# Linear attention and two feed-forward layers: the attention's two products in column halves

## The chip, the cores and the metric

The kernel runs on one core of a Trainium2 chip. The metric is the time of one execution on the device, in microseconds (us). The engines are named as the profile names them: PE is TensorE's matmuls and PEld its weight loads, DVE is VectorE, ACT is ScalarE, POOL is GpSimd, and SP is SyncE, which here only issues DMAs.

## What is computed

Attention with random features, with 4 sequences of 576 tokens, 8 heads of 64 and 128 features, then two feed-forward layers over the 2304 tokens, all of it in 32-bit floats:

```python
def phi(x):
    proj = np.einsum('bhsd,md->bhsm', x, omega)
    sq = np.sum(x * x, axis=-1, keepdims=True) / 2.0
    h = proj - sq
    h = h - np.max(h, axis=-1, keepdims=True)
    return np.exp(h) / np.sqrt(m)
q_p, k_p = (phi(q_s), phi(k_s))
kv = np.einsum('bhsm,bhsd->bhmd', k_p, v)
z = np.sum(k_p, axis=2)
num = np.einsum('bhsm,bhmd->bhsd', q_p, kv)
den = np.einsum('bhsm,bhm->bhs', q_p, z)[..., None] + 1e-06
return (num / den).astype(np.float32)
```

Then x is normed, goes through a gated layer (512 to 1536 to 512) and through a layer with h * cos(h) (512 to 2048 to 512). The two products that this case is about are kv with its sum z (from the keys' features and the values) and num with den (from the queries' features and kv).

## The kernel before

The 2304 tokens are 18 tiles of 128. A sequence has four and a half tiles, so tiles 4 and 13 each lie across two sequences; `parts(t)` gives the one or two pieces of a tile with their sequence, first partition and length.

A key tile goes this way. SyncE loads the transposed keys (`kraw`) and the values (`v`, one of three tiles, each 8 heads of 64 columns and one more column block that holds ones). `project` multiplies the keys by omega with two heads beside each other, in the upper and the lower 64 rows of the array (8 pairs of matmuls). `features` takes the maxima (DVE) and the exponentials (ACT, eight of them). `kv_product` then multiplies each head's features (stationary, 128 columns) by that head's values and the ones (moving, 64 + 64 columns), summed over a sequence in two banks of PSUM; `keep_kv` copies 65 of the 128 columns of each head to `kv`.

A query tile goes through eight steps, which `query_step` numbers: the projection and features, 1 the transposition of the features (`transposed`), 2 the products with kv (`sums`) and the division (`quotients`), 3 and 4 the mean square, 5 the norm, 6 and 7 the transposition into the layout of the first layer. In `sums` the transposed features of a head are stationary, and 128 columns of `kv` are moving, of which 65 are used later; a tile across two sequences does it in two halves of 64 tokens, each with its own `kv`.

The order on every engine is written out by hand: the program is a list of slots, and each engine does its instructions in the order in which the program issues them. In the key stage a slot s begins one tile (`begin(s)`) and does what older tiles are due for (`older(s, ...)`, whose arguments are the steps in their order; a key product has the number 1). There are 24 slots, with 18 key tiles and six query tiles. In the query stage the slots are the half steps of the first group of the first layer (`product`, `silu`, `gated`, `out1`), between which the remaining twelve query tiles are done.

Beside this the weights are prepared. They come as 64-bit floats and are turned into two parts of 32-bit words each: `front` makes a 32-bit value (its last step is an addition on POOL, L209), `high` casts its upper part (ACT, L214) and `low` subtracts it from the value (POOL, L217). The 12 pieces of the first group are made by `run` and `early_back`, while `self.early` is true; that ends with the key stage, and what is left of the twelve by then goes on with `self.early` false. `early_back` also asks for the piece after next but one, by a DMA from ACT's queue, right behind `high`.

Of the kernel before, what the change touches and what calls it, by code (L numbers as in the profile page):

```python
# [56 lines left out]
def attention_then_ffn(ctx: ExitStack, tc: tile.TileContext, qT, kT, v, omT, wc1, rms_g, wc2, out, B, H, S, D):  # L57
# [16 lines left out]
    IDLE = 9  # L74
    KVW = H * (D + 1) + D
    G = 4
# [50 lines left out]
    class Weights:  # L127
# [85 lines left out]
        def high(self, src, t, to):  # L213
            nc.scalar.copy(t[:, 0, to], src)  # L214

# [189 lines left out]
    class Attention:  # L405
# [51 lines left out]
        def sums(self, t, r):  # L457

            eT = self.eT.pop((t, r))
            ps = bank(self.tag, f"num_ps{t}_{r}")  # L460
            for h in range(HP):
                for b, p0, n in parts(t):
                    at = (2 * h + r) * (D + 1)
                    nc.tensor.matmul(
                        ps[p0:p0 + n, h * P:(h + 1) * P], eT[:, h, p0:p0 + n], self.kv[b][:, at:at + P],
                        start=True, stop=True, skip_group_check=True)
            self.ps["num", t, r] = ps
# [77 lines left out]
    with tc.manual_schedule():  # L545
# [20 lines left out]
        vp = values.enter_context(tc.tile_pool(name="values", bufs=1, side="right", reuse_waits="tile"))  # L566
        vt = [vp.tile([P, H + 1, D], F32, name=f"v{i}", bufs=1) for i in range(NV)]
        att = Attention(att_tile, "q", kv)
# [4 lines left out]
        def load_v(t):  # L573
            if t < NTILE:
                nc.sync.dma_start(vt[t % NV][:, 0:H], v[t])

        def kv_product(t, i):
# [3 lines left out]
            for r in range(2):  # L581
# [3 lines left out]
                for h in range(HP):  # L585
                    hh = 2 * h + r
                    nc.tensor.matmul(
                        acc[b, r][:, h * P:(h + 1) * P], att.e["k", t, r][p0:p0 + n, h, :],
                        vt[t % NV][p0:p0 + n, hh::H - hh, :],
                        start=begin and h == 0, stop=end, skip_group_check=True)  # L590
                if end:
# [199 lines left out]
        for a in vt:  # L791
            nc.vector.memset(a[:, H], 1.0)
        for a in kv:
            nc.vector.memset(a[:, H * (D + 1):], 0.0)
        make_identity(nc, ident)
# [4 lines left out]
        for s in range(SLOTS):  # L800
# [7 lines left out]
            begin(s)  # L808
            older(s, -7, -6, -4, -3, -2, -1, 1)
            if s:  # L810
# [138 lines left out]
        for n, (g, blk, f, first, last) in enumerate(steps):  # L949
# [13 lines left out]
            a = silu(blk, f, ps)  # L963
            older(s, -6, -4, -3, -2, -1)
            begin(s)
# [14 lines left out]
            hid[n] = gated(blk, f, a, ps)  # L980
            older(s + 1, -6, -4, -3, -2, -1)
            begin(s + 1)
# [447 lines left out]
```

## Time and profile before

| | |
|---|---|
| median of 3 runs | 964.47 us (964.46 to 966.03) |
| the profiled execution | 963.77 us |
| its span, from the first to the last instruction | 961.9 us |
| PE busy | 949.2 us, 99% of the span |
| DVE, ACT, POOL busy | 712.3, 536.9, 416.4 us |
| granted clock of TensorE | 0.999 of full speed over the span |

The time of an execution has 1.9 us around the span. A busy PE is not PE at its peak: matmuls are pipelined and overlap, so that the busy time of a group has the end of its last matmul in it, and the distance from one start to the next tells what one costs. A 32-bit matmul stands in the trace as two passes, each with a weight load of its own, so 8 matmuls are a row of 16.

### The profile page before, as it was taken

The numbers are of one execution on the slowest core, as the hardware profiler recorded it, in microseconds if no ns is written. First come the engines' busy times: TensorE is split into PE (matmuls) and PEld (weight loads), VectorE is DVE, ScalarE is ACT, GpSimd is POOL, SyncE is SP. The second block draws the span as 40 slices with busy tenths as digits, with TensorE's granted clock in tenths as the row PEclk, the third lists the DMA queues.
The fourth block names the chain that finished last, engine by engine and source line by source line (L and its number), as shares of the span: only waits on it lengthen the run. The fifth ranks groups of instructions, "written<-read, shape, count | busy, mean of one in ns | idle before, by whom it ended". The sixth has DMA issues, their size and how long they took to land. (4 is left out here: it accounts for less than half of the span.)

```text
span 961.9 us, 16225 instructions
## 1 busy us (share of the span) xinstructions
PE 949.2 (99%) x5761; PEld 892.0 (93%) x5761; DVE 712.3 (74%) x1163; ACT 536.9 (56%) x1155; POOL 416.4 (43%) x377
## 2 busy tenths in 40 slices
PE   9999999999999999999999999999999999999998
PEld 8998999989999999999999998888888889899897
DVE  5786677778863686577686648997799777786766
ACT  7787776775543524354453545575656565464443
POOL 2133367657944867275764673320244221230000
PEclk9999999999999999999999999999999999999999
DMA  8555178778697898846989794967622758307554
GB/s 313 157 181 187 57 265 293 256 265 263 219 328 291 328 330 295 302 152 197 376 303 377 249 348 152 345 231 271 208 88 79 272 186 303 125 23 269 197 226 162
DMA packets 96082, 227.65 MB, mean 237 GB/s; under 512 B 9728, under 2 KB 45184, under 8 KB 96000
## 3 DMA queue, kind: packets, MB, share of 16 engines
q1 hardware_dynamic: 94704, 222.34, 66.1%
q10 hardware_dynamic: 1296, 4.26, 1.2%
q8 instruction: 46, 0.75, 0.3%
q14 instruction: 36, 0.29, 0.1%
HBM read 156.04 MB, written 70.52 MB: 236 GB/s over the span
## 5 line engine op out<-in xcount | busy, mean ns | idle before, releaser
L1251 PE MATMUL o_ps<-w,o 128*128 128x512 f32 x864 | 226.0, 393 | 0.6 <-DVE o L1054 0.6
L209 POOL TENSOR_TENSOR f<-f,raw 128x512 f32<-128x512 f32 x68 | 94.7, 1393 | 230.3 <-DVE raw L204 184.6
L1251 PEld LDWEIGHTS o_ps<-w,o 128*128 128x128 f32 x864 | 159.7, 188 | 24.5 <-DVE o L1054 1.1
L217 POOL TENSOR_TENSOR w<-b,w 128x512 fp32r<-128x512 f32 x88 | 115.5, 1318 | 135.4 <-ACT w L214 125.6
L831 PE MATMUL gv_ps<-xhl,w 128*128 128x384 f32 x576 | 107.9, 335 | 1.6 <-DVE gv L870 1.1
L831 PEld LDWEIGHTS gv_ps<-xhl,w 128*128 128x128 f32 x576 | 100.5, 188 | 2.1 <-DVE gv L870 1.4
L1150 PE MATMUL y<-t,w 128*128 128x384 f32 x576 | 102.1, 334 | 0.3 <-POOL w L217 0.3
L1150 PEld LDWEIGHTS y<-t,w 128*128 128x128 f32 x576 | 100.0, 188 | 0.6 <-POOL w L217 0.6
L1051 ACT CAST o<-turns 128x384 fp32r<-128x384 f32 x96 | 47.5, 513 | 93.3 <-DVE turns L1232 93.3
L1043 PE MATMUL Xh<-T,w 128*128 128x384 f32 x432 | 87.4, 337 | 1.5 <-ACT h L1196 1.5
L1043 PEld LDWEIGHTS Xh<-T,w 128*128 128x128 f32 x432 | 76.8, 188 | 9.7 <-ACT h L1196 4.0
L1043 PE MATMUL X<-T,w 128*128 128x384 f32 x432 | 80.9, 335 | 0.0
L1043 PEld LDWEIGHTS X<-T,w 128*128 128x128 f32 x432 | 75.3, 188 | 0.5 <-DVE r L1078 0.3
L214 ACT CAST w<-b 128x512 fp32r<-128x512 f32 x88 | 50.5, 580 | 31.2 <-DVE b L274 23.9
L1054 DVE TENSOR_TENSOR o<-turns,o 128x384 fp32r<-128x384 f32 x96 | 59.9, 638 | 8.5 <-ACT o L1051 8.1
L884 PE MATMUL y_ps<-t,w 128*128 128x384 f32 x288 | 60.8, 346 | 0.0
L1017 ACT ACTIVATE turns<-turns,half_pi 128x768 f32<-128x768 f32 (+1 forms) x50 | 45.7, 914 | 22.4 <-DVE turns L1221 22.3
L1043 PE MATMUL Yh<-B,w 128*128 128x384 f32 x288 | 58.0, 336 | 0.0
L1221 DVE SCALAR_TENSOR_TENSOR turns<-turns,r 128x768 f32<-128x768 int32 (+1 forms) x50 | 56.4, 1128 | 1.7
L1232 DVE TENSOR_TENSOR turns<-h,turns 128x768 f32<-128x768 f32 (+1 forms) x50 | 54.8, 1096 | 2.4 <-ACT turns L1017 2.4
L1043 PEld LDWEIGHTS Yh<-B,w 128*128 128x128 f32 x288 | 51.4, 188 | 4.2 <-ACT h L1196 0.4
L190 DVE TENSOR_SCALAR f<-W 128x512 int32<-128x512 int32 x68 | 45.1, 663 | 13.6 <-ACT W L182 6.5
(117 smaller groups left out, 1853.6 us busy)
## 6 DMA issues: line engine op xcount, KB each, us to landing
T<-T_dram SPq DMA_DIRECT2D x48, 768.0 KB, 6.9
raw<-wc SPq DMA_DIRECT2D x60, 512.0 KB, 4.9
B<-yh_dram SPq DMA_DIRECT2D x21, 768.0 KB, 5.7
kept<-f SPq DMA_DIRECT2D x56, 256.0 KB, 5.0
b<-kept SPq DMA_DIRECT2D x56, 256.0 KB, 5.1
B<-x_dram SPq DMA_DIRECT2D x15, 768.0 KB, 6.6
x_dram<-xhl SPq DMA_DIRECT2D x12, 768.0 KB, 5.8
s<-x_dram SPq DMA_DIRECT2D x24, 384.0 KB, 6.3
```

The source lines that it names most:

```text
L209: nc.gpsimd.tensor_tensor(f32(f), f32(f), rest, op=ALU.add)
L214: nc.scalar.copy(t[:, 0, to], src)
L217: nc.gpsimd.tensor_tensor(t[:, 1, to], src, f32(t[:, 0, to]), op=ALU.subtract)
L831: nc.tensor.matmul(o, w[i], x[j], start=n == 0, stop=n == len(terms) - 1)
L884: nc.tensor.matmul(yacc[blk][e], w[:, i, e * P:(e + 1) * P], t[:, j], start=first and i + j == 0, stop=last and j == 1)
L1043: nc.tensor.matmul(o, w[:, i, c + kk * P:c + (kk + 1) * P], x[:, j, kk], start=begin and n == 0, stop=n == 5, skip_group_check=True)
L1051: nc.scalar.copy(t[:, 0], a)
L1054: engine.tensor_tensor(t[:, 1], a, f32(t[:, 0]), op=ALU.subtract)
L1150: nc.tensor.matmul(acc[e], w[:, i, e * P:(e + 1) * P], t[:, j], start=f == fs[0] and i + j == 0, stop=f == fs[-1] and j == 1)
L1221: nc.vector.scalar_tensor_tensor(r, a, -TWO_PI_LO, b, op0=ALU.mult, op1=ALU.add)
L1232: at(mu, lambda: nc.vector.tensor_tensor(r, h, r, op=ALU.mult))
L1251: nc.tensor.matmul(oacc[blk][j], o[:, x, js], w[:, y], start=first and n == 0, stop=last and n == 2)
```

## The change

Four things are edited.

- Both products go in two column halves. In `sums` the stationary features of a head are cut into tokens 0 to 63 and 64 to 127, in every tile; in `kv_product` the 128 features are cut likewise. Each half writes its own 64 partitions of PSUM. The moving operand has 65 columns, the head's 64 and the one of the sum.
- For that the tile of values has 65 columns a head, the last of them ones: the load writes 64 of 65 columns of each head. The memsets of the columns behind `kv`, which are no longer read, fall away.
- `high` casts on POOL and no longer on ACT, as long as `self.early` is true.
- In `older(...)` the steps -2 and -1 change places, at three calls.

```diff
-    KVW = H * (D + 1) + D
+    KVW = H * (D + 1)
...
         def high(self, src, t, to):
-            nc.scalar.copy(t[:, 0, to], src)
+            if self.early:
+                nc.gpsimd.tensor_copy(t[:, 0, to], src)
+            else:
+                nc.scalar.copy(t[:, 0, to], src)
...
             for h in range(HP):
-                for b, p0, n in parts(t):
-                    at = (2 * h + r) * (D + 1)
+                at = (2 * h + r) * (D + 1)
+                for c in range(2):
+                    half_c = slice(c * P // 2, (c + 1) * P // 2)
+                    b = parts(t)[min(c, len(parts(t)) - 1)][0]
                     nc.tensor.matmul(
-                        ps[p0:p0 + n, h * P:(h + 1) * P], eT[:, h, p0:p0 + n], self.kv[b][:, at:at + P],
+                        ps[half_c, h * P:h * P + D + 1], eT[:, h, half_c], self.kv[b][:, at:at + D + 1],
                         start=True, stop=True, skip_group_check=True)
...
-        vt = [vp.tile([P, H + 1, D], F32, name=f"v{i}", bufs=1) for i in range(NV)]
+        vt = [vp.tile([P, H, D + 1], F32, name=f"v{i}", bufs=1) for i in range(NV)]
...
-                nc.sync.dma_start(vt[t % NV][:, 0:H], v[t])
+                nc.sync.dma_start(vt[t % NV][:, :, 0:D], v[t])
...
-                    nc.tensor.matmul(
-                        acc[b, r][:, h * P:(h + 1) * P], att.e["k", t, r][p0:p0 + n, h, :],
-                        vt[t % NV][p0:p0 + n, hh::H - hh, :],
-                        start=begin and h == 0, stop=end, skip_group_check=True)
+                    for c in range(2):
+                        half_c = slice(c * M // 2, (c + 1) * M // 2)
+                        nc.tensor.matmul(
+                            acc[b, r][half_c, h * P:h * P + D + 1], att.e["k", t, r][p0:p0 + n, h, half_c],
+                            vt[t % NV][p0:p0 + n, hh, :],
+                            start=begin and h == 0, stop=end, skip_group_check=True)
...
         for a in vt:
-            nc.vector.memset(a[:, H], 1.0)
-        for a in kv:
-            nc.vector.memset(a[:, H * (D + 1):], 0.0)
+            nc.vector.memset(a[:, :, D:], 1.0)
...
-            older(s, -7, -6, -4, -3, -2, -1, 1)
+            older(s, -7, -6, -4, -3, -1, -2, 1)
```

The first place is on PE in the key stage, where the sums of the first query tile (`num_ps`) stand between a projection (`qp_ps`) and a key product (`kv_ps`), before:

```order
L426 MATMUL qp_ps_1_547<-om,qraw_421 128x128
L464 MATMUL num_ps_0_570<-kv_97,eT_0_498 128x128 x4
L464 MATMUL num_ps_1_580<-kv_97,eT_1_505 128x128 x4
L587 MATMUL kv_ps_0_447<-v_105,ke_0_520 128x128 x4
L587 MATMUL kv_ps_1_452<-v_105,ke_1_527 128x128 x4
L426 MATMUL kp_ps_0_602<-om,kraw_465 128x128
```

and after, where the shapes behind the names are those of one matmul's output:

```order
L429 MATMUL qp_ps_1_607<-om,qraw_457 128x128
L469 MATMUL num_ps_0_630<-kv_97,eT_0_550 64x65 x8
L469 MATMUL num_ps_1_644<-kv_97,eT_1_557 64x65 x8
L594 MATMUL kv_ps_0_483<-v_105,ke_0_572 64x65 x8
L594 MATMUL kv_ps_1_492<-v_105,ke_1_579 64x65 x8
L429 MATMUL kp_ps_0_678<-om,kraw_517 128x128
```

Nothing has changed its place, and each row of four matmuls became one of eight, all in halves, from the first of `num_ps` to the last of `kv_ps`.

The second place is on PE in the query stage, where a query tile's sums stand between two whole matmuls of the first layer (`gv_ps` and `y_ps`), before:

```order
L831 MATMUL gv_ps_1_0_1431<-xhl_0_774,w_795 128x384 x2
L831 MATMUL gv_ps_1_0_1431<-xhl_1_775,w_795 128x384 x2
L464 MATMUL num_ps_0_1446<-kv_98,eT_0_1393 128x128 x4
L464 MATMUL num_ps_1_1456<-kv_98,eT_1_1400 128x128 x4
L884 MATMUL y_ps_0_0_0_1465<-t_0_1382,w_417 128x384
L884 MATMUL y_ps_0_0_1_1466<-t_0_1382,w_417 128x384
```

and after:

```order
L836 MATMUL gv_ps_1_0_1619<-xhl_0_874,w_895 128x384 x2
L836 MATMUL gv_ps_1_0_1619<-xhl_1_875,w_895 128x384 x2
L469 MATMUL num_ps_0_1634<-kv_98,eT_0_1581 64x65 x8
L469 MATMUL num_ps_1_1648<-kv_98,eT_1_1588 64x65 x8
L889 MATMUL y_ps_0_0_0_1661<-t_0_1570,w_453 128x384
L889 MATMUL y_ps_0_0_1_1662<-t_0_1570,w_453 128x384
```

Here too the order is the same, but the halves now stand with 128-column matmuls on both sides. Seven of the twelve whole tiles of this stage are followed by a projection in place of `y_ps`.

The third place is POOL's first work on weights, where `f` is the 32-bit value and `w` the tile of its two parts, before:

```order
L209 TENSOR_TENSOR f_239<-f_239,raw_139 128x512
L217 TENSOR_TENSOR w_283<-f_239,w_283 128x512
L209 TENSOR_TENSOR f_281<-f_281,raw_172 128x512
L217 TENSOR_TENSOR w_367<-f_281,w_367 128x512
L209 TENSOR_TENSOR f_365<-f_365,raw_201 128x512
```

and after:

```order
L209 TENSOR_TENSOR f_243<-f_243,raw_139 128x512
L215 CAST w_295<-f_243 128x512
L220 TENSOR_TENSOR w_295<-f_243,w_295 128x512
L209 TENSOR_TENSOR f_293<-f_293,raw_168 128x512
L215 CAST w_395<-f_293 128x512
L220 TENSOR_TENSOR w_395<-f_293,w_395 128x512
L209 TENSOR_TENSOR f_393<-f_393,raw_197 128x512
```

A cast has come between the addition and the subtraction of a piece; there are eight such casts, and as many are gone from ACT. On ACT the DMA for a later piece stays where the cast stood before it.

## Rows read from the trace of the kernel before

**Rows 1.** First part of the page: busy us (share of the span) xinstructions.
```profile
PE 949.2 (99%) x5761; PEld 892.0 (93%) x5761; DVE 712.3 (74%) x1163; ACT 536.9 (56%) x1155; POOL 416.4 (43%) x377
```

**Rows 2.** Busy time by stretch: length; PE, PEld, DVE, ACT, POOL; clock, DMA, GB/s.
```profile
0.00:4.00 4.00, 2.90 (x9) 1.20 (x9) 0.84 (x9) 1.49 (x2) 0.84 (x9) 1.00 0.55 165
4.00:21.00 17.00, 16.70 (x173) 15.50 (x173) 11.16 (x21) 13.07 (x45) 4.16 (x3) 1.00 0.96 347
21.00:64.00 43.00, 42.85 (x438) 39.39 (x438) 33.42 (x70) 35.36 (x120) 11.75 (x13) 1.00 0.57 180
64.00:89.00 25.00, 24.33 (x255) 22.31 (x252) 19.37 (x44) 20.95 (x70) 8.96 (x8) 1.00 0.67 212
89.00:256.00 167.00, 164.06 (x1185) 158.77 (x1184) 126.48 (x255) 114.59 (x254) 108.50 (x114) 1.00 0.66 225
```

**Rows 3.** Timeline of a cycle in the key stage: start, length, what.
```profile
32.45 2.05 PE L464 MATMUL num_ps<-kv,eT 128*128 128x128 f32 x16
...
34.34 1.95 PE L587 MATMUL kv_ps<-v,ke 128*128 128x128 f32 x16
...
36.22 1.16 PE L426 MATMUL kp_ps<-om,kraw 64*128 64x128 f32 x16
...
37.31 1.09 PE L444 MATMUL eT_ps<-ident,qe 128*128 128x128 f32 x8
```

**Rows 4.** Timeline of TensorE, tile across two sequences, then a key product.
```profile
85.12 1.98 PE L464 MATMUL num_ps<-kv,eT 128*64 128x128 f32 x32
87.03 2.05 PE L587 MATMUL kv_ps<-v,ke 128*128 128x128 f32 x16
```

**Rows 5.** Groups by line and shape, 0 to 200 us: sums.
```profile
L464 PEld LDWEIGHTS num_ps<-kv,eT 128*128 128x128 f32 x192 | 22.8, 191 | 0.5
...
L464 PE MATMUL num_ps<-kv,eT 128*64 128x128 f32 x64 | 3.9, 276 | 0.0
...
L464 PEld LDWEIGHTS num_ps<-kv,eT 128*64 128x64 f32 x64 | 3.5, 136 | 0.4 <-issue 0.2
```

**Rows 6.** Busy time in two cycles of three tiles, columns as in rows 2.
```profile
31.36:41.41 10.05, 10.05 (x105) 9.28 (x104) 6.55 (x15) 7.34 (x26) 0.19 (x1) 1.00 0.43 139
41.41:51.40 9.99, 9.92 (x101) 9.08 (x101) 8.01 (x17) 7.71 (x29) 1.81 (x2) 1.00 0.40 108
```

**Rows 7.** Groups by line and shape, 0 to 200 us: GpSimd and the cast.
```profile
L209 POOL TENSOR_TENSOR f<-f,raw 128x512 f32<-128x512 f32 x21 | 29.3, 1397 | 61.4 <-DVE raw L204 50.1 <-DMA v<-v 11.3
...
L214 ACT CAST w<-f 128x512 fp32r<-128x512 f32 x12 | 7.6, 637 | 5.6 <-POOL f L209 5.6
...
L634 POOL CAST s<-s 128x384 fp32r<-128x384 f32 x8 | 4.9, 611 | 0.0
```

**Rows 8.** Waits in 21 to 89 us: waiting, released by, us, times, longest.
```profile
POOL w L217 <- ACT w L214: 5.8, 6, 2.4
ACT ke L437 <- DVE kmx L435: 5.7, 6, 2.1
...
ACT w L214 <- POOL f L209: 2.5, 3, 1.3
```

**Rows 9.** Lines L575 and L621: SyncE's issues in ns, minimum, median, maximum; landing.
```profile
L575 SPq DMA_DIRECT2D v<-v x18: 327/328/432, 1.6 to 74.2; - x18
...
DMA to landing us min/median/max: 2.5/4.2/5.7
...
L621 SPq DMA_DIRECT2D s<-x_dram x24: 524/572/1507, 121.7 to 366.5; - x24
```

**Rows 10.** DMA queues, 21 to 64 us: packets, MB, share of 16 engines.
```profile
q1 hardware_dynamic: 3098, 5.63, 43.6%
```

**Rows 11.** The same for 0 to 3.5 us, the queue of the omega load.
```profile
q10 hardware_dynamic: 144, 0.07, 6.5%
```

**Rows 12.** Waits of TensorE's matmuls in 89 to 256 us.
```profile
PE gv_ps L831 <- DVE gv L870: 1.1, 1, 1.1
PE qp_ps L426 <- PE eT_ps L444: 0.9, 1, 0.9
```

More of the change, by code (lines that the diff above doesn't have):

```diff
@@ L963, in attention_then_ffn @@
             a = silu(blk, f, ps)
-            older(s, -6, -4, -3, -2, -1)
+            older(s, -6, -4, -3, -1, -2)
             begin(s)
@@ L980, in attention_then_ffn @@
             hid[n] = gated(blk, f, a, ps)
-            older(s + 1, -6, -4, -3, -2, -1)
+            older(s + 1, -6, -4, -3, -1, -2)
             begin(s + 1)
```

## The prediction

> **What bounds the kernel now.** I read the page's first part first: TensorE is busy 99% of the span, all others 74% or less [rows 1]. A share over the whole span hides stages, so next comes the table by stretch. The change touches two stretches: the key stage (0 to 89 us, where all key tiles and six query tiles are projected) and the query stage (89 to 256 us, where the other twelve query tiles run between the first group's matmuls); behind 256 us no instruction changes. In 21 to 64 us TensorE is busy 42.85 of 43 us, VectorE 33.4, ScalarE 35.4; in 64 to 89 us the three are at 24.3, 19.4 and 21.0 of 25; in 89 to 256 us TensorE has 164.1 of 167 and VectorE 126.5 [rows 2]. So TensorE ends last in both, but in the key stage the next engines are only some 20% behind it. In 4 to 21 us there is another limit: the DMA engines are at 0.96 [rows 2].
>
> **One product, before.** The timeline of TensorE shows a query tile's sums and a key tile's product behind each other: sums from 32.45, the product from 34.34, the next projection at 36.22 [rows 3]. A row of 16 is one tile's 8 products in two passes each. Both products use the array in one shape, so 32 passes and one change of shape take 3.77 us. The projection behind them (16 matmuls that use half the rows each, two beside each other) takes 1.09 us to the next work: 8 pairs and one change. If a pair costs as much as a whole pass, 24 passes are 2.68 us: 112 ns each, 1.79 us a product, and 0.19 us for a change of shape.
>
> **One product, after.** Each product becomes two, of 64 stationary columns and 65 moving ones. The trace has the halves already, with 128 moving columns: the tile that lies across two sequences puts its upper and lower 64 tokens into separate halves. There 32 matmuls take from 85.12 to 87.03, 1.91 us [rows 4], as long as 16 whole ones: the two halves run beside each other, a pair in 110 ns (1.98 less the last one's 0.28, over 15.5 pairs) [rows 4, 5]. Loading weights takes 191 ns for 128 columns and 136 for 64 [rows 5]: 55 ns per 64 columns, so this half of the work shrinks in step. What 65 moving columns take no row shows. Bound below: in proportion, 110 x 65/128 = 56 ns a pair. Bound above: 110, if something other than columns (starting four instructions for a pair) sets the pace. I take 60, near the lower end, since both weights and moving columns are halved and the pair's four starts are the only thing that is not. A product then takes 16 x 60 = 0.96 us and saves 0.83.
>
> The Trainium skill, TensorE: Matmul & The Clock Gate, section "Wait — 56ns, not 53.3ns?", says that matmuls never start closer than about 25 ns, however small. If loads counted likewise, four starts would take 100 ns a pair by an estimate from that page, and the kernel would come out at about 963. The pairs here, with two matmuls and two loads in 110 ns, neither show nor exclude that.
>
> **The key stage.** Behind 21 us there lie 15 key products and 5 sums (counted in the order of TensorE: 20 key products in all, as two tiles lie across two sequences, 5 of them before 21 us). 20 x 0.83 = 16.6 us less on TensorE. The new shape adds 11 changes of shape, nearly all at the tiles across two sequences; a change into or out of the halves should cost a little under 0.19 (half the weights to load, a shorter last matmul), I take 0.17: 1.9 us. The rest, about 15, would bring TensorE from 67.2 to 52 us in these 68. But now the others count. ScalarE has 35.4 + 21.0 = 56.3 [rows 2] and loses 6 of the 8 casts that move (the other two come earlier), 0.64 each [rows 7]: 52.5. VectorE stays at 33.4 + 19.4 = 52.8 [rows 2]. So three engines stand at 52 to 53 us. Cycle by cycle it is the same: two cycles of three tiles, 10.0 us each, hold 7.3 to 7.7 us of ScalarE and 6.6 to 8.0 of VectorE [rows 6]. Today the bounding engine reaches 99% because the others have slack; three equal engines in fixed order, each handing on to the next (VectorE's maximum, ScalarE's exponentials, TensorE's product), won't. ScalarE already waits 5.7 us for VectorE's maxima here [rows 8]. I take 90% of the largest: 52.8 / 0.9 = 58.7, a gain of **9.3 us**. Bounds: at 100% 15.2, at 80% (66.0) 2.0.
>
> **The casts.** 8 of the first group's 12 casts move from ScalarE (637 ns) to GpSimd; the rest come when the key stage is over. A GpSimd cast of 384 columns takes 611 ns, so 815 for 512 [rows 7]. GpSimd's own work lies on both sides of it (1397 ns before, the subtraction behind). Before, GpSimd waited 5.8 us for this cast [rows 8], so its chain hardly grows: the cover is its idle time, 47 of 68 us [rows 2]. Were that gone, the norm's short operations, which stand in the same queue, would be late, and VectorE behind them, by up to a cast (0.8 us) a tile. ScalarE's wait for GpSimd's sum, 2.5 us [rows 8], stays: the DMA issue that stood behind the cast waits for the same sum. The other order of the steps -1 and -2 moves nothing: no slot holds both, and the rows of TensorE stand in the same order. The memsets left out are some 0.1 us each on an engine that then waits for a DMA: nothing.
>
> **The values' loads.** The tile is now 65 wide, so a load of 256 KB goes to 8 pieces of 256 bytes in each partition, where it was one of 2 KB. Issuing a load with one piece a partition takes SyncE 0.33 us, with two 0.52 to 0.57 [rows 9], so about 0.2 for each more: 1.7 us with eight. SyncE's queue holds the next tile's load behind it. Tiles are asked for three ahead and values some 7 us before use (a load takes 4.2 us to land [rows 9]), which hides 1.4 us. On the DMA engines: 5.63 MB took 43.6% of 16 x 43 us [rows 10], 0.87 us for a tile on all sixteen. That is the lower bound. Upper: 144 packets, 128 of them of 512 bytes, took 6.5% of 16 x 3.5 us [rows 11], 25 ns each; 1024 pieces at this price are 1.6 us. 512 bytes is the nearest row; I take 20 ns, 1.3 us, 0.4 more a tile. Behind 21 us thirteen tiles make 5 us on DMA engines that are busy 41 of 68: hidden. In 4 to 21 us, at 0.96, it isn't: the five tiles there add 2 us of transfers while the engines could go 1.5 us faster. Since most of those transfers are weights and tiles fetched ahead, I take **0** for this stretch, with -1.5 and +2 as ends.
>
> The Trainium skill, DMA: Bandwidth & Descriptors, Specifications, wants 512 bytes or more, as less makes the DMA engines read, modify and write. It gives no price; if it doubles the 25 ns, rival 4 follows.
>
> **The query stage.** Twelve whole sums at 0.83 make 10.0 us, and the one across two sequences, already in halves, saves 16 x 50 ns = 0.8. Against that the halves stand between whole matmuls: seven of the twelve (counted in the order) are followed by a projection, before which the shape changed anyway (one more each), five by whole matmuls (two more): 17 x 0.17 = 2.9. Net 7.9. TensorE is the bound with the others far below, and its 2.9 us of waiting are mostly for VectorE and for one transposition [rows 2, 12]; such waits come a little sooner when TensorE is quicker. I take **7.0**; ends 5 and 8.5.
>
> **Sum.** 963.77 (the profiled execution) - 0 - 9.3 - 7.0 = 947.5. The median shown is 0.7 above that execution, so I forecast 948, with 944 to 952 as the case's own range. A difference under 0.2%, 2 us, can't be told from none here.
>
> **Rivals.**
> 1. *The key stage follows TensorE better*: the three engines run at 97%, 54.5 us, 13.5 gained, and 7.5 in the query stage: 943. For it: ScalarE's and VectorE's waits today are mostly for TensorE. Against: equal loads.
> 2. *The key stage hardly gains*: a chain from projection to exponentials, or late values, takes the place of TensorE; 2 us there, 6 in the query stage: 956. For it: the waits for maxima [rows 8] and values that come with less lead.
> 3. *The halves don't get quicker* (the change doesn't do what it says): a pair stays at 110 ns, by the rate of starting instructions. Nothing is saved and 28 changes of shape cost 4.8: 969, slower. It decides from 103 ns a pair on: 33 products x 16 x 9 ns saved are 4.8. For it: no stretch of the trace starts four instructions in less than 110 ns for long. Against: none is built so that it could.
> 4. *The small pieces bound the key stage*: at 50 ns a piece (twice the 512-byte packet) a tile takes 3.2 us, 18 tiles 42 us more; with the 60 of today (0.55, 0.96, 0.57 and 0.67 of the four stretches [rows 2]) this is 102 us in a stage of 89: +13, less 7 later: 970, slower. It decides from about 33 ns a piece on, where transfers would fill what the three engines need (about 80 us with the start).
>
> **Chances.** Forecast 0.42, rival 1 0.17, rival 2 0.21, rival 3 0.09, rival 4 0.06; 0.05 between them near no change. Faster 0.83 (forecast, 1, 2 and a part of the last), same 0.06, slower 0.11. The range reaches from rival 1 to past rival 2, with mixtures of 2 and 3: 942 to 961.
>
> **What would show it.** Right: sums and key products with 64 columns in about 1.2 us a row of 32, weight loads at 136 ns; key stage ending near 80, the query stage near 240; VectorE and ScalarE at nine tenths in the key stage, TensorE now with waits for exponentials. Wrong: pairs at 100 ns or more (3); waits for the DMA of the values or SyncE busy with their issue, and DMA share near 0.95 through the key stage (4); an unchanged end of the key stage with idle TensorE (2). It would also be wrong if GpSimd's casts were far above 0.8 us and VectorE waited for the norm.

## The result: 955.3 us, 9 us faster, with most of the saved matmul time lost again in waits

| | before | changed |
|---|---|---|
| median | 964.47 us (964.16 to 966.03, 4 runs) | 955.31 us (954.37 to 958.52, 4 runs) |
| ratio | | 0.9908, 95% interval 0.9882 to 0.9934 |
| profiled execution, its span | 963.77, 961.9 us | 954.37, 952.6 us |

The forecast was 948 us. The page's first part of the changed kernel, against [rows 1]: 576 more matmuls and 21 us less of a busy TensorE, so that the span could have lost 21 us and lost 9.3.

```profile
PE 927.8 (97%) x6337; PEld 865.6 (91%) x6337; DVE 715.7 (75%) x1159; ACT 532.3 (56%) x1147; POOL 422.4 (44%) x385
```

The timeline of TensorE in the cycle of [rows 3] gives the price of one product: sums from 32.19, the key product from 33.17, the next projection at 34.20.

```profile
32.19 1.15 PE L469 MATMUL num_ps<-kv,eT 128*64 128x65 f32 x32
33.17 1.10 PE L594 MATMUL kv_ps<-v,ke 128*64 128x65 f32 x32
34.20 1.16 PE L429 MATMUL kp_ps<-om,kraw 64*128 64x128 f32 x16
```

16 pairs of halves take 0.98 us from one start to the next, 61 ns a pair, where 16 whole passes took 1.89 [rows 3].

Where the 21 us went is seen by cutting both traces at the same places: the first matmul of the query stage (`gv_ps`, at 88.84 before and 82.73 after) and the first of the paired layer behind it (at 298.06 and 289.17). The windows of before (length; PE, PEld, DVE, ACT, POOL busy; clock, DMA share, GB/s):

```profile
4.00:88.84 84.84, 83.73 (x858) 77.04 (x857) 63.95 (x132) 69.21 (x232) 24.87 (x24) 1.00 0.68 223
88.84:298.06 209.22, 206.28 (x1432) 200.80 (x1430) 151.75 (x302) 129.45 (x286) 127.99 (x130) 1.00 0.71 245
```

and of the changed kernel:

```profile
4.00:82.73 78.73, 68.43 (x1242) 59.97 (x1241) 66.39 (x126) 63.09 (x220) 31.60 (x32) 0.96 0.83 241
82.73:289.17 206.44, 200.61 (x1624) 191.48 (x1622) 153.29 (x308) 130.93 (x291) 127.10 (x130) 0.99 0.71 248
```

| stretch | TensorE's busy time | its idle time | length |
|---|---|---|---|
| key stage | -15.3 | 1.1 to 10.3: +9.2 | -6.1 us |
| query stage | -5.7 | 2.9 to 5.8: +2.9 | -2.8 us |

In each stretch busy and idle time add up to the length. The remaining 0.4 us of the span came behind these stretches, where nothing changed. In the key stage TensorE now waits for the others: its longest waits from 4 to 83 us (waiting, released by: us, times, longest), where the same view of before had only two entries, of 1.0 us together.

```profile
PE kv_ps L594 <- DMA v<-v: 2.6, 2, 1.8
PE kp_ps L429 <- ACT ke L440: 2.1, 1, 2.1
...
PE qp_ps L429 <- ACT ke L440: 1.5, 1, 1.5
...
PE kv_ps L594 <- ACT ke L440: 1.2, 2, 0.9
PE kp_ps L429 <- DVE eT L457: 1.0, 1, 1.0
```

And TensorE's clock, at 2.4 GHz before until the last microseconds, now falls three times to 1.2 GHz, for 3.41 us each (at 17.7, 58.6 and 202.0). The windows around two of the falls:

```profile
55.50:58.60 3.10, 0.99 (x12) 0.80 (x14) 3.07 (x5) 1.82 (x8) 2.96 (x3) 1.00 0.62 205
58.60:62.01 3.41, 3.41 (x46) 3.07 (x46) 3.35 (x8) 3.38 (x12) 1.18 (x4) 0.51 0.43 131
...
198.50:202.00 3.50, 1.33 (x15) 0.93 (x15) 2.09 (x6) 1.78 (x6) 3.25 (x5) 1.00 0.87 314
202.00:205.41 3.41, 3.41 (x18) 3.19 (x15) 3.39 (x5) 2.95 (x8) 3.25 (x4) 0.50 0.73 267
```

Each fall follows a wait of TensorE: 1.8 us from 16.0, 2.1 us from 55.9 and 1.7 us from 198.8.

### The profile page after: what moved, and what is told of

Same layout as the page of the kernel before. It is cut to its first block, busy times and chain, and to the rows that moved or that the text cites. A ratio compares the mean times of both kernels' runs of the same rounds, so it can differ in the third digit from the quotient of the medians.

```text
span 952.6 us, 17378 instructions
## 1 busy us (share of the span) xinstructions
PE 927.8 (97%) x6337; PEld 865.6 (91%) x6337; DVE 715.7 (75%) x1159; ACT 532.3 (56%) x1147; POOL 422.4 (44%) x385
```

## The experiments

In all of them, before is the kernel before on the same chip (965.2 to 965.3 us). Ratios are to it, with 95% intervals. One caution holds for all: the key stage doesn't end at the same time in every execution. Three kernels with the same code in it (the changed one, `put_first` and `put_once` below) left it at 82.73, 84.99 and 86.24 us in their profiles, so single profiles tell its length only to some 3 us.

A part of this is TensorE's clock. The stage's last projection goes on at 79.62, 80.33 and 81.60 us in the three, and behind it TensorE has no wait left. The changed kernel needs 3.1 us from there to the end, the others 4.7 and 4.6. TensorE's last sums and last key product there, in the changed kernel and then in `put_once`, with the clock of the latter's stretch:

```profile
80.71 1.15 PE L469 MATMUL num_ps<-kv,eT 128*64 128x65 f32 x32
81.69 1.10 PE L594 MATMUL kv_ps<-v,ke 128*64 128x65 f32 x32
82.73 1.51 PE L836 MATMUL gv_ps<-xhl,w 128*128 128x384 f32 x7
```
```profile
82.80 2.00 PE L469 MATMUL num_ps<-kv,eT 128*64 128x65 f32 x32
84.59 1.72 PE L594 MATMUL kv_ps<-v,ke 128*64 128x65 f32 x32
86.24 2.03 PE L836 MATMUL gv_ps<-xhl,w 128*128 128x384 f32 x10
```
```profile
82.80:86.24 3.44, 3.44 (x66) 3.37 (x65) 3.30 (x11) 3.42 (x12) 0.00 (x0) 0.55 0.28 107
```

A fall of the clock at this place costs 1.5 us. It is there in the profiles of `put_first`, `put_once`, `act_cast` and `padded_values`, and not in the changed kernel's.

### Where the casts are made

**e1, act_cast.** The changed kernel with the casts back on ScalarE.

```diff
         def high(self, src, t, to):
-            if self.early:
-                nc.gpsimd.tensor_copy(t[:, 0, to], src)
-            else:
-                nc.scalar.copy(t[:, 0, to], src)
+            nc.scalar.copy(t[:, 0, to], src)
```

> The changed kernel with one part undone: the first group's upper parts are cast by ScalarE again. Theory A (GpSimd's casts lengthen VectorE's instructions, and VectorE bounds the key stage): VectorE's two instructions that grew, the mask of the raw words (667 ns in the mean, 423 before) and the norm (1730, 1257 before), fall back, the key stage ends 2 to 4 us sooner than 82.7 us, and the kernel is at 951 to 954 us. Theory B (the forecast: ScalarE stands as high as VectorE, so its 5.2 us of casts count): the key stage ends 2 to 5 us later, 957 to 960 us.

955.19 us, ratio 0.9900 (0.9886 to 0.9913): the same as the changed kernel, so neither. Its key stage ended at 84.21 us, 1.5 later, but the last projection goes on at 79.57 in it and at 79.62 in the changed kernel; the rest is the clock's fall at the end. In the key stage ScalarE is busy 69.0 us in place of 63.1 (5.2 of it the eight casts) and VectorE 65.3 in place of 66.4, although this window holds six more of VectorE's instructions. The groups of two of VectorE's lines show what the casts on GpSimd cost it. In the changed kernel, 4 to 82.73 us (busy us, mean ns of one):

```profile
L497 DVE SCALAR_TENSOR_TENSOR x<-x,ms,gain 128x512 f32<-128x512 f32 x4 | 6.9, 1731 | 0.2 <-POOL ms L493 0.2
L195 DVE TENSOR_SCALAR raw<-f 128x512 int32<-128x512 int32 x9 | 6.0, 667 | 0.1
```

and in e1:

```profile
L494 DVE SCALAR_TENSOR_TENSOR x<-x,ms,gain 128x512 f32<-128x512 f32 x4 | 5.9, 1476 | 0.2 <-POOL ms L490 0.2
L195 DVE TENSOR_SCALAR raw<-f 128x512 int32<-128x512 int32 x9 | 4.8, 529 | 0.1
```

Before, the two took 1257 and 423 ns. The Trainium skill, SBUF — State Buffer, Terms, says that VectorE and GpSimd share a pair of ports that one of them holds for a whole instruction. The trace agrees: of the nine masks the median still takes 425 ns in the changed kernel and the longest 1377, so that a few are held up and not all slowed. That it is the ports that hold them no run here shows.

**e2, late_ask.** ScalarE's queue asks for the weight piece after next but one behind GpSimd's subtraction, no longer behind the cast. In the changed kernel that request waits for GpSimd's addition: at 56.40 it is issued, and the exponentials behind it start at 56.78, after 2.35 us in which ScalarE did nothing.

```diff
         def early_back(self, c):
-            for i in self.split(self.f.pop(c), self.todo[c]):
-                self.load(c + 3)
+            for n, i in enumerate(self.split(self.f.pop(c), self.todo[c])):
+                if n == 1:
+                    self.load(c + 3)
                 yield
```

> The changed kernel with one thing moved: ScalarE's queue asks for the weight piece after next but one behind GpSimd's subtraction, not right behind the cast. Theory C (ScalarE's waits, which the trace puts down to VectorE's maxima, are the DMA issue in its queue that waits for GpSimd's addition; 2.35 us at 56 us): ScalarE's waits in the key stage shrink by 4 us or more, the longest waits of TensorE for exponentials go, the clock falls at most once, and the kernel is at 950 to 953 us. Rival (VectorE bounds the stage, so ScalarE's waits cost nothing): 954 to 957 us, no change.

955.04 us, ratio 0.9897 (0.9884 to 0.9911): no gain, although the clock doesn't fall once before the end of this execution:

```profile
4.00:83.13 79.13, 67.47 (x1242) 59.09 (x1241) 66.90 (x127) 63.38 (x220) 31.62 (x32) 1.00 0.81 239
83.13:289.92 206.79, 199.46 (x1625) 190.12 (x1622) 154.21 (x308) 131.17 (x291) 127.27 (x130) 1.00 0.71 248
```

TensorE is busy 1.0 and 1.2 us less than in the changed kernel, and idle 1.4 and 1.5 us more. So the changed kernel's three falls of the clock cost next to nothing: what TensorE lost by them it would have waited anyway. The fall at the end of the key stage, shown above, does cost. Nor does the late request keep the clock up by itself: in e10, which has it too, the clock stood at 1.2 GHz for 6.8 us from 24.2 and again from 65.1 us. Its waits are now for VectorE rather than for exponentials:

```profile
PE kv_ps L595 <- DVE kv L606: 2.2, 2, 1.6
PE kp_ps L430 <- DVE eT L458: 2.2, 2, 1.2
PE kp_ps L430 <- DVE xhl L522: 1.8, 2, 1.3
```

### The loads of the values

**e3, padded_values.** The values lie in memory with their columns of ones, so that a load has one piece of 2080 bytes a partition and not eight of 256.

```diff
-                nc.sync.dma_start(vt[t % NV][:, :, 0:D], v[t])
+                nc.sync.dma_start(vt[t % NV], v[t])
...
-        for a in vt:
-            nc.vector.memset(a[:, :, D:], 1.0)
...
```

> The changed kernel with the values' load in one piece of 2080 bytes a partition: the tensor in memory already holds a column of ones beside each head's 64 values, laid there when the inputs are arranged, so the memsets are left out too. Theory D (1024 pieces a load hold up the start: key products wait for values, SyncE's issues are held up to 2.9 us): the waits of TensorE for the values' DMA (2.6 us) go, the tenth projection starts 1 to 2.5 us sooner, no fall of the clock at 17.7 us, 952 to 954 us. Rival (the start is bound by bytes, not by pieces): the waits stay, 955 us within 1.

956.53 us, ratio 0.9908 (0.9893 to 0.9923). The rival had the time right: the small pieces cost nothing that can be measured. But it had the waits stay, and they went. TensorE waits for no load of values in this key stage, where the changed kernel had waited 2.6 us for them, all of it ahead of 18 us; the projection that began at 34.20 us there still begins no earlier (34.95).

### The two products apart

**e4, sums_only** (the kernel before with the edit of `sums` alone) **and e5, keys_only** (the changed kernel with the casts on ScalarE and the old `sums`, with its wide `kv`). The edit of `sums` in e5, from the changed kernel; e4 has the reverse, from the kernel before:

```diff
...
-                at = (2 * h + r) * (D + 1)
-                for c in range(2):
-                    half_c = slice(c * P // 2, (c + 1) * P // 2)
-                    b = parts(t)[min(c, len(parts(t)) - 1)][0]
+                for b, p0, n in parts(t):
+                    at = (2 * h + r) * (D + 1)
                     nc.tensor.matmul(
-                        ps[half_c, h * P:h * P + D + 1], eT[:, h, half_c], self.kv[b][:, at:at + D + 1],
+                        ps[p0:p0 + n, h * P:(h + 1) * P], eT[:, h, p0:p0 + n], self.kv[b][:, at:at + P],
...
```

> The kernel before with one part of the change: only the queries' sums go in halves with 65 moving columns; key products, values' load and casts as before. By the forecast's prices: the query stage gains 0.5 to 0.6 us for each of 13 tiles, 7.0 us in all, the key stage 5 x 0.5 or so, and the kernel is at 955 to 957 us. Rival (the query stage can't give more than the 2.8 us seen in the changed kernel, as waits for VectorE and for loads take the rest): 960 to 962 us.

> Before, with the values' tile of 65 columns and the key products in column halves; the sums stay whole matmuls of 128 columns and the casts stay on ScalarE. The sums alone gave 7 us and both together 9 to 10. If the two parts add, the key products are worth 2 to 3 us here: 961 to 963, with the query stage as long as before, and the key stage ending 2 to 4 us earlier although TensorE's key products take some 17 us less in it. The rival is that the key products alone give all that the key stage gained in the changed kernel (6 us), and the sums gave their part only after it: then 958 to 959.5.

Sums alone: 957.99 us, ratio 0.9930 (0.9916 to 0.9943), between the two expectations and nearer the forecast's. Keys alone: 960.81 us, 0.9946 (0.9934 to 0.9958). The key stage, cut as above, in e4 and then in e5:

```profile
4.00:85.82 81.82, 80.27 (x921) 73.54 (x921) 63.68 (x130) 68.29 (x231) 24.90 (x24) 1.00 0.70 232
```
```profile
4.00:83.83 79.83, 71.24 (x1178) 62.88 (x1177) 64.83 (x129) 67.99 (x231) 24.98 (x24) 0.98 0.82 238
```

The sums take 3.5 us from TensorE there and give 3.0; the key products take 12.5 and give 5.0; both, with the same casts (e1), take some 16 and give 4.6, or 6.1 without the clock's fall at the end. Each is a single profile, with the spread above, so 5.0 and 6.1 can't be told apart. That the stage gives far less than TensorE's 12.5 or 16 us is clear all the same: it follows TensorE for the first 3 us and then much less. In e4 the query stage was 3.9 us shorter than before (205.36 us), so that the sums alone had gained 6.9 us at its end, the changed kernel 8.9. Another 1.8 us were lost in e4 far behind, at 352.7 us, where TensorE waited for VectorE. The keys' gain came out at 4.5 us by the medians, above the 2 to 3 expected: by the key stage alone the rival was nearer.

### What makes a pair quick

**e6, whole_65.** The changed kernel with whole matmuls of 128 stationary columns, but 65 moving ones.

The edit of the key products (that of the sums is likewise):

```diff
...
-                    for c in range(2):
-                        half_c = slice(c * M // 2, (c + 1) * M // 2)
-                        nc.tensor.matmul(
-                            acc[b, r][half_c, h * P:h * P + D + 1], att.e["k", t, r][p0:p0 + n, h, half_c],
-                            vt[t % NV][p0:p0 + n, hh, :],
-                            start=begin and h == 0, stop=end, skip_group_check=True)
+                    nc.tensor.matmul(
+                        acc[b, r][:, h * P:h * P + D + 1], att.e["k", t, r][p0:p0 + n, h, :],
+                        vt[t % NV][p0:p0 + n, hh, :],
+                        start=begin and h == 0, stop=end, skip_group_check=True)
```

> The changed kernel with both products as whole matmuls again, of 128 stationary columns (halves only in the tiles across two sequences), but with 65 moving columns. If the moving columns alone set the price (A), a product of 16 rows takes 0.98 us as the halves do, 61 ns a row, and the time is that of the changed kernel, 954 to 957. If a whole weight load takes a row's place as it did before (B), a row stays at 117 ns, a product at 1.88 us, and all of the gain is lost: 963 to 967. In between, at 85 ns a row, about half is lost: 958 to 961.

982.88 us (973.86 to 986.54), ratio 1.0175 (1.0140 to 1.0210): B for the row, and a time worse than B's. The timeline of TensorE, key product to the next projection:

```profile
34.36 2.00 PE L590 MATMUL kv_ps<-v,ke 128*128 128x65 f32 x16
36.29 0.94 PE L429 MATMUL qp_ps<-om,qraw 64*128 64x128 f32 x12
```

1.93 us: a whole row costs the same with 65 moving columns as with 128 [rows 3]. The clock makes it slower than before. In the fastest of its runs, the profiled one, it stood at 1.2 GHz for 6.8 us from 27.3 and for 10.2 from 78.5:

```profile
18.50:27.30 8.80, 8.78 (x91) 8.45 (x91) 7.46 (x12) 5.55 (x19) 5.68 (x7) 1.00 1.02 294
27.30:34.10 6.80, 6.80 (x46) 6.12 (x46) 2.48 (x4) 4.76 (x17) 1.21 (x1) 0.50 0.72 206
70.00:78.50 8.50, 8.50 (x79) 8.05 (x79) 7.14 (x16) 6.37 (x24) 4.54 (x5) 1.00 0.57 155
78.50:88.70 10.20, 10.20 (x62) 9.52 (x62) 4.01 (x8) 3.66 (x13) 2.58 (x4) 0.50 0.81 254
```

17.0 us at half speed are 8.5 us, and its key stage ended 8.35 us later than that of before (97.19). Here the falls cost their full price, as TensorE was the bound. The two fastest runs have a clock of 0.991 and 0.987 of full speed over the span, the other four, at 982.85 to 986.54 us, one of 0.972 to 0.978.

**e11, halves_128.** The kernel before with both products in halves, but 128 moving columns. The edit of the sums (that of the key products is likewise):

```diff
-                for b, p0, n in parts(t):
-                    at = (2 * h + r) * (D + 1)
+                at = (2 * h + r) * (D + 1)
+                for c in range(2):
+                    half_c = slice(c * P // 2, (c + 1) * P // 2)
+                    b = parts(t)[min(c, len(parts(t)) - 1)][0]
                     nc.tensor.matmul(
-                        ps[p0:p0 + n, h * P:(h + 1) * P], eT[:, h, p0:p0 + n], self.kv[b][:, at:at + P],
+                        ps[half_c, h * P:(h + 1) * P], eT[:, h, half_c], self.kv[b][:, at:at + P],
...
```

> The kernel before with both products in column halves, but still with 128 moving columns; loads, casts and everything else as before. If the price of a row goes by its moving columns and two halves share the time of a whole (A), a product of 32 rows takes what 16 whole rows took, 1.9 us, as the sums of a tile across two sequences did in the kernel before, and the time is that of before, 963.5 to 967. If twice as many instructions with weight loads of their own cost more (B), at 70 ns a row a product takes 2.2 us and the 36 products lose some 11 us: 970 to 978.

966.33 us, ratio 1.0012 (1.0003 to 1.0021): A. The timeline of TensorE:

```profile
32.30 1.98 PE L466 MATMUL num_ps<-kv,eT 128*64 128x128 f32 x32
34.10 1.92 PE L591 MATMUL kv_ps<-v,ke 128*64 128x128 f32 x32
35.95 1.16 PE L426 MATMUL kp_ps<-om,kraw 64*128 64x128 f32 x16
```

1.80 us a product, 112 ns a pair, and the query stage took 212.21 us in place of 209.22. That 3.0 is what the halves cost there without a quicker pair. Changes of shape are most of it: a gated product ahead of sums takes 2.18 us to the next start for 2.08 before, and sums ahead of `y_ps` 1.90 for 1.70, so 0.10 into the halves and 0.20 out of them; at the places where they are new this makes 2.2. The key stage was 0.7 shorter.

### What bounds the key stage

**e8, few_weights.** The changed kernel without the first group's weight work in slots 6 to 23; what is missing is made at the start of the query stage.

```diff
-                wts.tick(5 if s < 6 else 1 if s < 14 else 4 if s + 1 < SLOTS else 0)
+                wts.tick(5 if s < 6 else 0)
```

> The changed kernel with no weight work in slots 6 to 23 of the key stage; it is all made up at the start of the query stage, so only the time up to the last key product is to be read, and the whole time is longer. If what VectorE, ScalarE and GpSimd do for the weights is what keeps the key stage from following TensorE (A), the last key product ends 4 us or more earlier than in the changed kernel, at 76 to 79 us, and TensorE's waits for exponentials shrink. If it is the loads of the values and the chain from projection to exponentials alone (B), it ends less than 2 us earlier, and the waits for the values stay.

1003.35 us in one run, as the weights are missing later. The last key product was over at 77.3 us, 5.4 earlier than in the changed kernel: theory A.

```profile
4.00:77.30 73.30, 66.80 (x1241) 58.33 (x1240) 53.88 (x108) 59.88 (x214) 13.51 (x17) 1.00 0.79 224
```

VectorE has 12.5 us less to do there, GpSimd 18.1, ScalarE 3.2, and TensorE's idle time fell from 10.3 to 6.5 us. The edit relieves them all at once, so it doesn't tell which of them the stage had waited for.

### The stall at 200 us

The last term that the prediction missed is in the query stage: from 198.8 to 200.5 us TensorE stood still behind a transposition, for 1.7 us, where the kernel before had lost 0.9 us (at 208.6). TensorE's timeline, before and then in the changed kernel (idle time ahead in brackets; "issue" is a wait for nothing that the profile shows):

```profile
207.53 1.03 PE L444 MATMUL eT_ps<-ident,qe 128*128 128x128 f32 x8
209.50 0.46 PE L426 MATMUL qp_ps<-om,qraw 64*128 64x128 f32 x2 [0.93 <-PE eT_ps L444]
```
```profile
197.74 1.04 PE L447 MATMUL eT_ps<-ident,qe 128*128 128x128 f32 x8
200.52 0.46 PE L429 MATMUL qp_ps<-om,qraw 64*128 64x128 f32 x2 [1.74 <-issue]
```

**e7, deep_queries.** A fourth buffer, and query tiles asked for three ahead.

```diff
-        depth = {"gain": 1, "raw": 3, "feat": 3, "mx": 6, "den": 4}
-        with_keys = {"raw": 1, "feat": 2}
+        depth = {"gain": 1, "raw": 4, "feat": 3, "mx": 6, "den": 4}
+        with_keys = {"feat": 2}
...
-        keys[0], AHEAD[0] = False, 2
+        keys[0], AHEAD[0] = False, 3
```

> The changed kernel with a fourth buffer of its own for the transposed queries, so that in the query stage a query tile is asked for three tiles ahead and not two. If the stall of 2.0 us at 198 to 200 us, where TensorE waits for a query tile's load, is a load that was asked for too late, it goes, and with it the fall of the clock behind it (1.5 us): 952 to 953.5. The rival is that SyncE's queue and the DMA engines are full there, so that another load comes late in its place, or the order of the queue sets the wait: 954.5 to 956.

956.06 us, ratio 0.9907 (0.9891 to 0.9922); the stall stood where it was (1.8 us, up to 201.82). So the wait isn't the load. VectorE's timeline of the changed kernel shows it:

```profile
199.33 0.43 DVE L190 TENSOR_SCALAR f<-W 128x512 int32<-128x512 int32 x1 [3.59 <-ACT W L184]
199.67 0.75 DVE L521 TENSOR_TENSOR xhl<-xT_ps,xhl 128x256 fp32r<-128x256 f32 x2
```

The subtraction L521 is the last reader of the bank that the next projection (from 200.52) writes, and it stood in VectorE's queue behind a weight step that had waited 3.6 us for ScalarE. So it isn't the queue that the rival named either, which was that of the loads; e12 below bears this reading out.

**e9, put_first; e10, put_first with the edit of e2; e12, put_once.** The subtraction goes ahead of the weight steps in the whole query stage, or at the one slot.

```diff
-            wts.pace(rates[0], 0.0)
             older(s + 1, -7)
+            wts.pace(rates[0], 0.0)
...
-            wts.pace(rates[0], 0.0)
             older(s + 2, -7)
+            wts.pace(rates[0], 0.0)
```
```diff
+            if n == 12:
+                older(s + 1, -7)
             wts.pace(rates[0], 0.0)
-            older(s + 1, -7)
+            if n != 12:
+                older(s + 1, -7)
```

> The changed kernel with one exchange in the query stage: the last step of a query tile (the subtraction that makes the lower part of the transposed tile and frees its bank of PSUM) is issued ahead of the weights' steps and no longer behind them. Theory A: the stall of 2.0 us of TensorE at 198.5 to 200.5 us is VectorE's: the subtraction stands there behind a weight step that waits 3.6 us for ScalarE, and the next projection needs the bank. Then the stall goes, 2.0 us and the clock's fall behind it (1.7 us): 951.5 to 953.5. Theory B: the stall is a load or anything else than this order, and nothing changes: 954.5 to 956. Theory C: VectorE and ScalarE together bound these microseconds, and the wait only moves on to the next first-layer matmuls, as it did where the clock did not fall: 953.5 to 955.5, with the stall gone at its place and one of 1.5 to 2 us behind it.

> The exchange of the run before this one, and besides it a weight piece is asked for one step later, behind GpSimd's subtraction. Asking later took the clock's falls out of the key stage and left the time as it was. If the two add to nothing, the time is that of the exchange alone within 1 us. If the key stage gives what the clock took there (two falls of 3.4 us at half speed, 3.4 us at most), it is 1 to 3 us below the exchange alone: 949 to 952.

> The changed kernel with the exchange of the earlier run at one slot only, the one of the stall at 198.5 to 200.5 us: there alone VectorE subtracts the transposed tile's lower part ahead of the weight steps. Everywhere else the order is that of the changed kernel. Theory A: there the cast that the subtraction needs is done 1.5 us before the subtraction runs, so that nothing new waits; the stall of 2.0 us goes and the clock's fall behind it too: 951.5 to 953.5. Theory C: VectorE and ScalarE bound these microseconds, the stall goes at its place, and 1.5 to 2 us of it come back before the next tile's gated product, as in the run that asked for weights later: 953.5 to 955.5. If the time rises above 957, an order that is moved at one slot already costs what it cost at all of them.

e9: 968.92 us (967.63 to 969.41), 1.0034 (1.0022 to 1.0046). e10: 967.45 (964.87 to 970.39), 1.0024 (1.0014 to 1.0035), so that the late request adds nothing that can be told. None of e9's three theories had foreseen this: its query stage grew by 12 us, to 218.4. The groups of L521 there, in e9 and then in the changed kernel:

```profile
L521 DVE TENSOR_TENSOR xhl<-xT_ps,xhl 128x256 fp32r<-128x256 f32 x28 | 10.5, 417 | 15.7 <-ACT xhl L519 12.2 <-PE eT_ps L447 3.5
```
```profile
L521 DVE TENSOR_TENSOR xhl<-xT_ps,xhl 128x256 fp32r<-128x256 f32 x28 | 10.5, 416 | 4.6 <-ACT xhl L519 3.9 <-PE eT_ps L447 0.7
```

Ahead of the weight steps, the subtraction itself waits 11 us more, 8 of them for ScalarE's cast, and all of VectorE waits behind it. The weight steps had filled that time.

e12: 958.72 us, 0.9929 (0.9915 to 0.9943), 3.4 us above the changed kernel by the medians, though the intervals of the two ratios overlap. At the slot itself theory C held. TensorE's timeline (in this execution all is 3.2 us later):

```profile
202.22 0.46 PE L429 MATMUL qp_ps<-om,qraw 64*128 64x128 f32 x2 [0.24 <-PE eT_ps L447]
204.04 1.16 PE L429 MATMUL qp_ps<-om,qraw 64*128 64x128 f32 x14 [1.36 <-DVE gv L875]
```

The stall is gone and one of 1.4 us came in the middle of the projection, for the gated product that now stands later in VectorE's queue; from the sums ahead of this place to the next tile's took 18.04 us for 18.60, 0.6 won. Behind it 2.0 us were lost again by the start of the paired layer, in waits that the changed kernel had in part or not at all (1.5 us at 220.5, 0.5 there). The rest of the loss lies ahead of the edit: this execution left the key stage 3.5 us later than the changed kernel's, in code that is the same in both. 2.0 of them are there when the last projection goes on (81.60 for 79.62 us), behind a stop of TensorE at 33.4 us (below), and 1.5 are the clock's fall at the end. Whether all six of its runs had these, no profile shows.

No version tried beats the changed kernel.

## Why the prediction came out as it did

It was right in direction, and 955.3 lies in its range of 942 to 961, but outside the 944 to 952 of the forecast's own case: the gain is 9.2 us in place of 16.5.

- **A pair of halves: right.** 61 ns for the forecast 60. The estimate of 100 ns, made from the 25 ns a start of the Trainium skill, TensorE: Matmul & The Clock Gate, "Wait — 56ns, not 53.3ns?", by counting loads as starts too, fell; two matmuls in 61 ns agree with the 25 ns themselves. e6 and e11 show why both edges had to be cut: with 128 stationary columns a row costs the same with 65 moving columns as with 128, and with 128 moving columns a pair costs 112 ns. The prediction's reason, that weights and moving columns are both halved, was the one that counts. The Trainium skill, TensorE: Matmul & The Clock Gate, LDWEIGHTS (loading the stationary operand), gives the stationary columns divided by 1.2 GHz: 107 ns for 128 by its figure. The whole rows, 117 to 120 ns a pass, agree with such a bound; two loads of 64 one behind the other would be 107 ns again, so by that figure the pairs at 61 ns must have them overlap, which no run here shows by itself.
- **Changes of shape: right in the sum.** 17 x 0.17 = 2.9 us forecast for the query stage, 3.0 measured in e11, of which the rows of single changes (0.10 and 0.20) make 2.2.
- **First 21 us: 0, roughly right.** The fifth projection began 1.0 us later than before (19.78 for 18.76), within the bound of 2; in `put_once`, with the same code there, at 18.79.
- **TensorE's work in the key stage: a little large.** 25 products at 0.83 from 4 us on, less 1.9 for shapes, are 18.8; 16.3 measured where the clock held (83.73 to 67.47, e2).
- **Key stage: the mechanism right as far as shown, the size off.** -9.3 forecast, -6.1 measured. The term was VectorE's 52.8 us at 90%. VectorE came to 88% in 21 to 83 us (54.7 of 62), but its work had grown by 1.9 us, and 54.7 / 0.88 is 62 in place of 58.7. "VectorE stays at 52.8" is the step that failed. Its instructions had become longer: nine masks at 667 ns for 423 and four norms at 1731 for 1257 are 4.1 us, of which 2.3 come with the casts on its neighbour GpSimd (529 and 1476 ns in e1). The window shows less, as the last query tile's quotients now lie behind it. e8 shows that the weights' work holds the stage up (5.4 us), and e4 and e5 that the stage stops following TensorE after some 3 us. That among the engines it is VectorE is argued from its 88%, and no run shows it alone.
- **The casts: free, but not by the cover named.** GpSimd had the time, as forecast. They cost VectorE 2.3 us while ScalarE was relieved of 5.2, and the time came out the same (e1). That ScalarE's wait for GpSimd's sum stays was foreseen, and that it would then stop TensorE for 2.1 us wasn't; but e2, without it, is no faster.
- **Values' loads: free, as forecast, though not hidden.** TensorE waited 2.6 us for values in the first 18 us, where before it hadn't; without these waits the time is the same (e3). The issue takes 0.55 us in place of the 1.7 reckoned from one and two pieces, so the extrapolation was wrong and harmless.
- **Query stage: the step that failed.** -7.0 forecast, -2.8 measured. The work was about right: 6.8 us less on TensorE where the clock held (e2), for 7.9. But that the others are "far below" was read from a share of the stage. The 0.9 us put aside for waits became 2.9 of idle time and a fall of the clock, or 4.4 without the fall: the first layer's matmuls come sooner, and VectorE and ScalarE, in their fixed orders, do not. At one place, the stall at 198.8 us, e12 shows this; for the rest of the stage it is argued. Rival 2 had the time right (956), but by luck: by 2 us in the key stage and 6 in the query stage, where the chip gave 6.1 and 2.8.

Left open: why the clock falls at the end of the key stage in some kernels and not in others with the same code there, and what else sets the end of that stage up to 2 us apart.

## What to carry to other kernels

When the bounding engine is relieved in a fixed order, read the idle time of the others in each cycle and not over the stage: a 76% share of VectorE was already enough to give back more than half of a saving in the query stage. A matmul with few moving columns (65 here) paid only once its stationary part was cut as well, and the other way about. Moving a step forward in an in-order queue to end one wait moves all that stood ahead of it; where it ended a stall of 1.7 us at one place, done in the whole stage it cost 12 us. And one profile of a stage is one draw: kernels with the same code there were up to 3.5 us apart.

## What the hardware showed that was not expected

The clock fell while TensorE was busy 8.50 of 8.50 us (e6, at 78.5 us), so a wait ahead of it isn't needed; the rows there last as long as before and move 65 columns in place of 128. Why it falls, these runs don't settle, and not every wait was followed by a fall: in e2 TensorE stood for 1.7 us at 199.6 without one.

In e12 TensorE stopped for 1.9 us amid a key product, at 33.4 us, after 6 of its 32 rows. The trace shows nothing it waited for. A packet of 16 KB of the instruction queue came at 32.7 us, about 10 us behind the one before it. In the changed kernel these packets number 28 in the first 400 us, and 23 before. That TensorE waited for its own instructions fits, and wasn't tested.
